# Two attention blocks on one core: scores of a fourth tile ahead of the first values, another pace, a smaller mask, another loop order

## The chip, the core and the metric

The kernel runs on one core of one Trainium2 chip. PE multiplies matrices; VectorE, ScalarE and GpSimd work on vectors; SP issues the DMAs. The metric is the device time in microseconds, the median of several runs. The kernel before takes 1738.6 us (three runs, 1738.31 to 1740.38).

## The reference

Two blocks of attention, each with its own input x (2048 rows of 640) and weights, in float32, 32 heads of 20. Their outputs are put side by side.

```python
# block A: each row attends to 8 rows: itself and those 2, 4, ... 14 before it
idx = pos[:, None] - off[None, :]                 # off = 0, 2, ..., 14
logits = jnp.einsum("bhsd,bhswd->bhsw", q, kg) * scale
logits = jnp.where(mask, logits, -1e9)            # rows before the first are masked
o = jnp.einsum("bhsw,bhswd->bhsd", softmax(logits), vg);  outA = o @ wo
# block B: full attention
p = softmax(jnp.einsum("bhqd,bhkd->bhqk", q, k) * scale)
o = jnp.einsum("bhqk,bhkd->bhqd", p, v);  outB = o @ wo
```

## The kernel before

Every instruction goes through one helper (line 71) that keeps program order, so each engine runs its own instructions in the order in which the program emits them, and all rows of the profile have line 71.

**Stages.** First come block A's projections to q and k (to about 144 us), then block B's (to 281 us, 40 groups of 15 matmuls, lines 590 to 637), then the value projections of both blocks (lines 956 to 998, to about 457 us), during which the first maxima of block B are taken; then the loop over block B (lines 1114 to 1137, 488 steps), a tail of 24 steps, and the last outputs.

**Block A** (lines 329 to 430) has no matmuls in its attention: GpSimd does it. The 2048 rows are 16 tiles of 128. A tile has eight *units*: four of scores (`a_scores`: multiply by q, then add up by halves) and four of values (`a_values`). `UNITS` is the list of (tile, c) in order; c under 4 is a score unit. With `R_AHEAD` = 3 the scores of three tiles come before the first values. Between a tile's scores and values stands its softmax (`a_softmax`), a generator that is moved on by one step per unit (line 417); its maximum and reciprocal run on VectorE, its exponential on ScalarE. Each unit's rows are loaded two units ahead through SP into one of four `akv` buffers (`a_fetch`). Line 412 holds the generator in two cases: while one of the next three units needs value rows that aren't computed yet (`v_rows`), and at a tile's first value unit while two finished tiles wait (`done_a`). Finished tiles are taken from that list in `begin` (line 1033) alone, from step 11 of the loop on.

How much of block A's work is emitted when is set by a running estimate of GpSimd's time, `gp.us`, in which an operation costs 0.2 us and about 2 ns for each column. In the projection of block B, `a_pace` (line 494) is called after each group with `A_SLOW * QK_US * groups` (0.91 x 3.42 us a group), in the value stage with the stage's own estimate (2.2 or 2.72 us a tick), and the loop (line 1037) goes on by 2.36 us a step.

**Row maxima of block B** go through `max_rows` (line 642): VectorE reduces and turns them, GpSimd splits them into two parts (`mtr`), SP stores and loads them.

**The loop over block B** follows a string, `ORDER`. PSUM has eight banks of 512 columns. A token's letter says what is computed and its digits which banks are used. S: two halves of scores, whose exponentials ScalarE takes out of two banks. M: two products for row maxima, reduced by VectorE in one instruction over two adjoining banks (1024 columns). N: the same, reduced in two instructions of 512. Y: one half of scores and one product for maxima. V: one step of the weighted sum of values, every second time with a bank for it. H: a fifth of an output half tile of block A. j: one of five turns of a finished tile of block A on VectorE. A matmul into a bank waits until the instruction that last read that bank has ended.

Of the kernel before, what the change touches and what calls it, by code (L numbers as in the profile page):

```python
# [75 lines left out]
def attention_pair(ctx, tc, xa, wqk_a, wv_a, wo_a, xb, wqk_b, wv_b, wo_b, oa, ob):  # L76
    nc = tc.nc
    PS = bass.MemoryType.PSUM
    const = ctx.enter_context(tc.tile_pool(name="const", bufs=1))
# [937 lines left out]
    def begin(i):  # L1017
# [34 lines left out]
        "S20VY72M3S05Y61V7Y02S35N64VY03N21H65Y74H65S03H65Y72H65Y01H65Y43N72V0S13N46Y75VS41S72N36V0Y13M4S76VS71M2S46V0"
        "Y71S25M3VY71H62Y35H62Y01Y74H62Y35H62Y01H62M3Y75V0S16Y72N34VS15N76S23N40V1Y27S65N43VM6Y05S42V1Y04S73N26VN07S25"
        "H43Y61H43Y02H43Y57H43S06M1H43Y75V0Y16S24N35VY71S62M3Y50V1Y76M3S25VY07H65Y42H65Y70Y13H65Y42H65Y70H65N41V2Y03S74"
        "M5VjM0S73Y46V5jS70jM1S36VY70S14M2V6jS75jM0Y23VY75S04M1S36N75V0S14M2Y76VY15S74M2S60N15V7S64M2Y01VY64S05M2S17N64"
        "V0S15Y23M6VY15M3S27S06N15V2Y70M3S16VY70Y16S53S42N70V1M5S73Y04VM5S72Y34V0Y17S26N54VY71S62Y35Y40Y17V6M2S05Y74VM2"
        "S01H45Y76H45Y03Y21H45Y67H45Y03H45M1Y76V0S53Y74Y12VM3S72Y56V1S07M3Y26VY07M3S25Y61V0S72M3Y56VY71S25M3Y60V7S15M3"
        "Y62VY01M3S56Y27V0Y16M3S52VY71M5S24H03H03Y71H03Y24Y56H03Y71H03S24M5V7Y03S21N65VY06S14M2Y57V6S01jM2Y45VY70M2S14"
        "S56Y70jV1jM2S45Y06VM2S74Y56V0jY71M2jS46VY71M4S63S20N17V6Y52S13Y04VM1S73Y45V0Y17S62N35VY71S64M2S50N17V6Y52M3S01"
        "VY70S15S24N36N07V1S26Y53Y04VM2S75Y46V0Y71S23N65VY74M1S36S50N47V3Y26M4S01VY07M1S64S35N70V6S14M2Y75VY04Y73H21Y65"  # L1060
        "H21S04H21Y37H21Y06H21M4S73N60V2S17M4S36VM0Y73S45V6Y70S12M3VY70S15Y42N36V7S05M1Y34VY06S51M2Y47V0Y16S52M3VY71H26"
        "N35S04H26Y71H26Y03H26Y54H26M0S73V5Y46S70M1VY74S06M1Y35V4Y07M1S63VY07M5S31Y24V7S03jM5Y12VY03M5S41S27Y03jV4jM5"
        "S12Y37VM5S02Y17V3jY04M5jS72VY70S14M5S23N07V1S26Y05M3VS72M5S04Y31V7Y06Y52Y14VN06S53M1S47Y05V6Y43M1S70VY75M3S02"
        "S16N57V0Y14M2S56VY71M4S63S02Y17V6M4S70Y32VM4S70Y12V3Y47M5S02VY70S14M5S23N07V1Y26S05N43VS07Y62H54N31H54S02H54"
        "Y37H54Y60H54M1S73V0S46M1S75VM3S72Y16V5Y07M3S62VY07S61M3Y25V7Y60M3S12VY06M1S53Y47V6Y50S13N24VS70Y15H23N46H23S75"
        "H23Y40H23Y17H23M5Y04V7Y31M5S02VY04M1S35S67N40V3Y21M5S47VY04M1S75Y63V0jS74jM1S56jVjM3S75Y21V6jY70M3S51VY70M1S35"
        "S46N07V3Y24M0S56VY72M4S60S31N27V6Y05M2S41VY70M4S13S26Y07V1M4S72Y36VM4S07Y62V3Y04S75Y21VM0S74Y56V2Y73M0S46VY73"
        "S45Y06N12Y73V4S05Y61N72VS03M5S71Y42V0Y73M5S12VY71M3H25S60H25Y17H25N63S40H25Y17H25S64N03V1Y02M5S73VY07S24M5Y31"
        "V7Y02S64Y53VM0S26Y34V5Y70M1S64VY07S63M1Y45V7Y60M1S34VY06M3S52Y17V6Y05S42N31VM3S70H52Y16H52Y73Y40H52Y16H52Y73"
        "H52M0S46V7Y52S34M0VY62S35S04N17V6jM2S51Y70VjM2S14Y05V7jY61S23M4VjY06M1S35S47jY60V3M1S45Y07VM1S46Y75V0Y14M2S56V"  # L1070
        "Y71S64M2S50N17V6Y52M3S01VY70M1S53S46N07V5Y41M2S06VY70Y61M2S45Y07V6Y51M2S04VY70Y15S42M6Y03S15V4M6S02Y31VS07M5"
        "Y13V2Y04M5S71VY70M3S15Y62V0Y17M3S56VY71M5S24H30H30Y71H30N24S56H30Y71H30S25N64V7Y60M2S14VY06S15M2S47V6Y01S52M3V"
        "M0S75Y43V2Y01M6S35VY01S35Y74Y62V1M3S02Y57VN06S24H73H73M0S25H73Y46H73H73M0S25N46V7S03M1Y45VS06M3S21Y75V0Y62M3"
        "S15VY71S62M3V5jY70S61M3VY07S62S13M4jV0jM6S25jY14jVM6S53Y21V4Y03M6S52VY05M2S71S64N50V7Y61S25M3VY06M1S53S74N60V5"
        "Y71S62M3VY07M1S63S45N70V6Y14S73N52VY70M4S31S26N70V3S24Y51M6VY04M1S57S63Y04V5Y67M1S43VY07S64M1S35V7Y60S41M2VN06"
        "S54H32H32M0S75H32Y46H32H32M0S75Y64V3Y70M1S45VM6S04Y51V2Y03Y74S56VM0S73Y45V6Y70M1S53VY70S54M1H36H36Y70H36Y45Y21"
        "H36Y70H36M4Y21V7S06M2Y45VY06S14M2Y57V0Y16M2S45VY71M4Y63S02V1Y07M4S62VY07M2S64Y51V7Y06M2S45VY06M4S13Y27V6S01jM4"
        "Y32VY70S15M3S26Y70jV1jM3S25Y06VS72jM3jM5S01S72Y34V0Y17M5S42VY71S43M5S20N17V4Y35M1S06VY07M5S31S42N70V3Y41M5S72V"
        "Y70M1S46S35N07V4Y36M1S05VY07M5S31S42N70V3S41M5Y72VS04M5S71N23V0S74M5Y12VY73S41Y56N02V7S61M3Y05VS61M3Y02S57V6M3"
        "S01Y52VM3S70H12H12Y56H12Y07Y34H12Y56H12S07M3V5Y62S01Y43VY07S61M2V4Y05S76M2VY70S15M2Y64V0Y71M2S56VY71M5S42Y30V1"  # L1080
        "Y74S25N63VY07M5S42H31H31Y07H31Y24Y56H31Y07H31M4Y26V0S71M2Y45VY71M2S46S50V7Y61M2S45VjM0S64Y32V5jY06S71N42VY07M3"
        "S61S25jY70V6jM3S21Y05VY74M2jS15V0Y74S16M2VS71M4S63Y20V7S61M4Y03VM1S64Y50Y37S62Y14N05V3S42M6Y01VY24M6S05Y13V2"
        "Y04M6S15VY01M3S57Y62V0S17M3Y56VY71S25M3Y60V7Y15M3S62VY06M1S53S74N60V5Y71S62M3VY07M1S63S45N70V6S14M2Y75VY04Y73"
        "H21Y65H21S04H21Y37H21Y06H21M4S73V0Y12S74M5VS71M2S46Y50V7Y41M2S06VY51S04M2V6Y75S01M2VY70M4S31Y26V0Y73M4S12VY71"
        "M2S64H50H50Y17H50Y64Y32H50Y17H50M3Y62V1S07M5Y43VY07M5S42Y31V0Y72M5S43VjS74jM1S35Y06V7jY14M2S65VY04S16M2V5jY74"
        "S01M2VY07jS61M2S45Y70V6M2S41Y05VY74M2S15V0Y74S16M2VY71S64M2S50Y71V6Y52S43N01VY70Y52S43M0S76Y25V4Y37S01M5VY73"
        "S02M5V1Y73S04M5VY07M2S46S51N70V4Y35M6S21VY05M1S37S64N50V3Y27M5S41VY70M1S46Y35V0Y74S16M2VS71Y64H52N03H52S74H52"
        "Y60H52Y71H52M3S06N17V5S04M2Y61VS07M2S46N15V0S74Y32Y16VM4S73Y62V1Y07M4S32VY07S63M4Y21V7Y06M4S32VY06M2S14H57H57"
        "Y60H57Y41Y23H57Y60H57M1Y43V6S70M4Y12VY70S15M3Y26V7Y05M3S21VY02M5S14S73Y20jV1jY74M5S03VjY72S04M5V3jY72M0jS65V"
        "Y72S64M0S53N27V6Y05S41N23VY70N15Y42S36V7S01S34M5VM0S23Y65V4S70M1Y35VS07M1S36Y54V0Y71M2S46VY71S45M2S60N17V4Y35"  # L1090
        "S62M0VY73M5S20S14N37V2Y01M5S34VY70M3S15S26N07V1M3Y02S56VY07M3H56S21H56Y70H56Y24Y31H56H56N70S42Y31V5Y40S67M1V"
# [114 lines left out]
```

## Time and profile before

| | |
|---|---|
| median of three runs | 1738.6 us (1738.31 to 1740.38) |
| profiled execution, from first to last instruction | 1736.3 us |
| PE busy | 1724.5 us (99%) |
| VectorE busy | 1348.7 us (78%) |
| ScalarE busy | 1338.9 us (77%) |
| GpSimd busy | 1266.2 us (73%) |
| granted TensorE clock, mean | 0.999 of full speed |
| mean DMA rate | 143 GB/s |

The page gives no other time of the profiled execution than its span. In the profile DVE is VectorE, ACT is ScalarE, POOL is GpSimd, PEld is PE's loading of weights. Matmuls are pipelined and their ends are modelled, so a busy PE isn't PE at its peak; what PE waits for is seen best at its weight loads. A group's busy time leaves out overlaps between its instructions, its mean does not.

### The profile page before, as it was taken

The page shows a single profiled execution, that of the slowest core. Times are in us where ns is not written, and L with a number is a line of the kernel's source. Part 1 is how long each engine was busy: PE and PEld are TensorE (multiplying, and loading weights), DVE is VectorE, ACT ScalarE, POOL GpSimd, SP SyncE. Part 2 cuts the span into 40 slices and gives each one's busy share as a digit, 9 for nine tenths or more (in the row PEclk, how much of TensorE's full clock was granted, in tenths as well). Part 3 has the DMA queues.
Part 4 walks back from the last instruction along what each step waited for, and adds up shares of the span by engine and source line. Part 5 has one row for each costly group of instructions (what it writes and reads, how often), then busy time and mean ns, then how long its engine had stood idle before and what let it go on. Part 6 is the DMA issues. An engine that isn't in the chain of part 4 may idle for free.

```text
span 1736.3 us, 34687 instructions
## 1 busy us (share of the span) xinstructions
PE 1724.5 (99%) x12711; PEld 1006.0 (58%) x12711; DVE 1348.7 (78%) x1825; ACT 1338.9 (77%) x2658; POOL 1266.2 (73%) x1122
## 2 busy tenths in 40 slices
...
GB/s 227 119 139 239 304 261 273 259 204 187 199 151 125 96 161 153 93 136 158 135 95 173 126 119 127 170 135 88 158 143 106 147 95 61 46 36 53 33 76 113
DMA packets 194436, 248.29 MB, mean 143 GB/s; under 512 B 89309, under 2 KB 114397, under 8 KB 193273
## 3 DMA queue, kind: packets, MB, share of 16 engines
...
## 4 chain that ended last, share of the span: by engine, by line
PE 90%; POOL 4%; DVE 2%; ACT 1%; DMA 1%; issue 1%; SPq 0%; POOLq 0%; ACTq 0%; DVEq 0%
PE ps_st L71 90%; POOL akv L71 2%; DVE mx L71 1%; ACT e L71 1%; POOL xn L71 1%; DMA stg<-wv_b 0%; SPq L71 0%; POOL ww L71 0%; POOL xl L71 0%; POOL ao L71 0%; ACT more L71 0%; DMA vb_d<-ve 0%; POOL al L71 0%; DMA s_d<-sm 0%; DMA rb<-s_d 0%
## 5 line engine op out<-in xcount | busy, mean ns | idle before, releaser
L71 DVE TENSOR_REDUCE mx<-ps_st 128x1 f32<-128x512 f32 (+1 forms) x1504 | 1227.6, 875 | 57.3 <-PE ps_st L71 47.8
L71 ACT ACTIVATE e<-ps_st 128x512 f32<-128x512 f32 x2048 | 1066.7, 627 | 30.7 <-PE ps_st L71 16.8
L71 PE MATMUL ps_st<-bk,bq 60*128 60x512 f32 x2048 | 553.4, 436 | 1.0 <-ACT ve L71 0.5
L71 PE MATMUL ps_st<-bq,bk 62*128 62x512 f32 x2048 | 548.7, 433 | 5.6 <-ACT ve L71 3.0
L71 PE MATMUL ps_st<-e,vb 128*32 128x512 f32 x4096 | 543.0, 604 | 0.4
L71 PEld LDWEIGHTS ps_st<-bq,bk 62*128 62x128 f32 x2048 | 274.8, 184 | 403.3 <-ACT e L71 246.5
L71 POOL TENSOR_TENSOR braw<-braw,more 128x512 f32<-128x512 f32 x224 | 288.2, 1287 | 85.5 <-ACT more L71 85.1
L71 PEld LDWEIGHTS ps_st<-bk,bq 60*128 60x128 f32 x2048 | 257.1, 184 | 108.7 <-DVE mx L71 61.2
L71 POOL TENSOR_TENSOR akv<-akv,aq 128x1280 f32<-128x1280 f32 x64 | 188.9, 2951 | 166.4 <-DVE w L71 166.3
L71 POOL TENSOR_TENSOR akv<-akv 128x640 f32<-128x640 f32 (+3 forms) x304 | 282.2, 928 | 14.4
L71 ACT COPY ro<-ps_st 128x320 f32<-128x320 f32 (+2 forms) x172 | 73.7, 463 | 171.1 <-PE ps_st L71 122.7
L71 PE MATMUL ps_st<-ww,xn 64*128 64x320 f32 (+1 forms) x1776 | 187.1, 309 | 0.0
L71 PEld LDWEIGHTS ps_st<-ww,xn 64*128 64x128 f32 (+1 forms) x1776 | 175.7, 186 | 14.6 <-ACT e L71 8.3
L71 PEld LDWEIGHTS ps_st<-e,vb 128*32 128x32 f32 x4096 | 82.1, 108 | 149.0 <-issue 75.4
L71 POOL TENSOR_TENSOR akv<-akv,al 128x1280 f32<-128x1280 f32 x64 | 151.6, 2368 | 0.2
L71 ACT COPY more<-ps_st 128x512 f32<-128x512 f32 x224 | 136.3, 609 | 3.5 <-PE ps_st L71 1.5
L71 PE MATMUL ps_st<-xn,w 128*128 128x512 f32 x480 | 115.8, 390 | 0.0
L71 PEld LDWEIGHTS ps_st<-xn,w 128*128 128x128 f32 x480 | 90.1, 188 | 19.3
L71 ACT CAST pr<-ps_st 128x512 fp32r<-128x512 f32 x40 | 23.5, 587 | 98.8 <-PE ps_st L71 96.0
L71 PE MATMUL ps_st<-ww,aot 64*128 64x320 f32 x960 | 99.7, 308 | 0.0
L71 DVE TENSOR_TENSOR pr<-ps_st,pr 128x512 fp32r<-128x512 f32 x40 | 27.6, 691 | 86.7 <-ACT pr L71 86.7
L71 PEld LDWEIGHTS ps_st<-ww,aot 64*128 64x128 f32 x960 | 90.3, 186 | 5.8 <-POOL ao L71 0.6
...
## 6 DMA issues: line engine op xcount, KB each, us to landing
akv<-ka_d SPq DMA_DIRECT2D x128, 320.0 KB
akv<-va_d SPq DMA_DIRECT2D x128, 320.0 KB
...
rb<-s_d SPq DMA_DIRECT2D x128, 64.0 KB
```

The costliest lines, as they stand in the source:

```text
L71: return self.tc.keep_in_program_order(op(*a, **k))
```

## The change

The list `UNITS` has the scores of four tiles (16 units) before the first values; from tile 2's values on it is as before. For that the buffer `al` of scores has four copies in place of three, and the mask is kept once for all heads and broadcast in the addition. While the unit's index is under `EARLY` = 16, each softmax takes two steps per unit. `A_SLOW` is 0.78. The string `ORDER` is another one with as many steps (V 488), S-halves (1952) and maxima products (1840); H stands at the same steps, j mostly one step earlier. S goes from 625 to 634 tokens, M from 440 to 349, N from 129 to 229, Y from 702 to 684.

```diff
@@ -50,7 +50,7 @@
 AHEAD = 2.4
 QK_US = 3.42
 V_US = 2.72
-A_SLOW = 0.91
+A_SLOW = 0.78
 A_FROM = 1
 
 
@@ -310,10 +310,10 @@
         pe.transpose(warm[:, :128], ident, ident)
     give(warm)
 
-    mask = const.tile([128, WIN, H], F32, name="mask")
+    mask = const.tile([128, WIN], F32, name="mask")
     gp.memset(mask, 0.0)
     gp.affine_select(out=mask, in_=mask, compare_op=ALU.is_ge, fill=NEG, base=-PAD,
-                     pattern=[[1, WIN], [0, H]], channel_multiplier=1)
+                     pattern=[[1, WIN]], channel_multiplier=1)
     ones = [sb.tile([128, 16 * VC + 11], F32, tag=tag, bufs=3 if tag == "raw" else 2, name="ve")
             for tag in ("raw", "rb", "raw", "rb")]
     for t in ones:
@@ -326,7 +326,10 @@
 
 
 
-    UNITS = [(t, c) for k in range(NT + R_AHEAD) for t, cs in ((k - R_AHEAD, range(4, WIN)), (k, range(4))) if 0 <= t < NT for c in cs]
+    EARLY = 4 * R_AHEAD + 4
+    UNITS = [(t, c) for t in range(R_AHEAD + 1) for c in range(4)] + [
+        (t, c) for k in range(R_AHEAD, NT + R_AHEAD) for t, cs in ((k - R_AHEAD, range(4, WIN)), (k, range(4)))
+        if R_AHEAD < t < NT or cs[0] for c in cs]
     v_rows = [0]
     a_kv, a_t = {}, {}
 
@@ -351,7 +354,7 @@
 
     def a_scores(t, c, kv):
         if c == 0:
-            a_t[t][1] = sb.tile([128, WIN, H], F32, tag="al", bufs=R_AHEAD, name="al")
+            a_t[t][1] = sb.tile([128, WIN, H], F32, tag="al", bufs=R_AHEAD + 1, name="al")
         q, L, _ = a_t[t]
         pool(kv, kv, q.unsqueeze(1).to_broadcast([128, 2, D]), ALU.mult)
         yield
@@ -364,7 +367,7 @@
 
         _, L, _ = a_t[t]
         if t % (NT // 2) == 0:
-            pool(L, L, mask, ALU.add)
+            pool(L, L, mask.unsqueeze(2).to_broadcast([128, WIN, H]), ALU.add)
         yield
         yield
         m = sb.tile([128, 4, H], F32, tag="am", bufs=2, name="am")
@@ -415,7 +418,8 @@
             for d in done_a:
                 d[0] -= 1
             for g in soft.values():
-                next(g, None)
+                for _ in range(2 if n < EARLY else 1):
+                    next(g, None)
             if c == 4:
                 run_jobs(soft_jobs, 1)
                 for _ in soft.pop(t):
@@ -1044,66 +1048,67 @@
 
 
     ORDER = (
-        "Y07S61M2Y45V0Y71S26M3Y05V7Y06M3S52Y71V0Y26M3S75VY71M5S24S03N17V2Y06S15Y34VM0S74Y56V3Y70S21N46VY70M4S12S63N07V1"
-        "Y26M4S03VY07M2S64S51N70V6Y52S73N41VY70S52M3Y16V7Y05S42Y31VM4S06Y12V3jY07M4S26VjY70M1S64S53V0M6S14Y25VjM6S13M4"
-        "S20V1jY27S63jM4VY07M2S64S51N70V6Y52M3S71VY70M1S53S46Y07V5jM1S74Y63VjM1S07M3S65S02jY71jV6jM3S50Y12VM3Y70S52V1"
...
-        "S31N70V2S36M4Y71VY03M4Y76S12V0Y71M4S32VY71M2Y64S05Y17V6Y05M2S41VY70Y15S42Y36S07N15V4M1S36Y50VM1S73Y06")
+        "S51N24N73Y60V5Y17Y64Y02S53V1Y03M6S45Y21V0Y43M5S27VY31S24M6S05N31V2S04Y76Y35VM0S46Y57V3Y14N20S67VY42M6S15S03N42"
+        "V1Y06M4S73VY07M2S64S51N07V6S45M2Y10VY75M3S12Y06V7Y52S14Y03VjM5S32Y41V0jY56N37S21VY25S61M3S07V2jM5S13Y04VM6S13"
+        "M4jS20V1Y27S63M4VjY20M3S65S17N20V6Y13M4S27VY30M1S76S54Y30jV7jY12M5S40VY23Y41S75jS60M2Y41V7M5S32Y01jVM4Y26S31j"
...
+        "S72M5Y40V1Y32M5S70Y34VS23M6N51S04V2S36Y07M4VS31M6Y03S25N41S67V0M3S26Y15VM3S71Y06")
```

## Rows read from the trace of the kernel before

**Rows 1.** Windows view: busy us of each engine in stretches, then granted clock, DMA share, GB/s

```profile
core 0: us, PE busy (x) PEld busy (x) DVE busy (x) ACT busy (x) POOL busy (x), PEclk, DMA share, GB/s
...
470.00:1600.00 1130.00, 1127.94 (x8412) 510.60 (x8408) 1100.99 (x1543) 1098.26 (x2202) 995.84 (x879) 1.00 0.42 120
...
240.00:303.00 63.00, 63.00 (x354) 55.33 (x354) 21.55 (x29) 22.66 (x38) 3.81 (x8) 1.00 0.84 272
...
400.00:450.00 50.00, 46.56 (x541) 42.72 (x538) 38.82 (x38) 10.89 (x25) 48.51 (x35) 1.00 0.68 207
```

**Rows 2.** Waits view, 470 to 1600 us: total us, times, longest us

```profile
DVE mx L71 <- PE ps_st L71: 18.5, 66, 1.0
...
ACT e L71 <- PE ps_st L71: 16.5, 48, 0.9
...
PEld ps_st L71 <- ACT e L71: 314.2, 506, 0.9
...
PEld ps_st L71 <- DVE mx L71: 170.3, 346, 0.9
```

**Rows 3.** Timeline, GpSimd, 235 to 302 us: start, us, instructions, [idle before <- releaser]

```profile
235.78 2.96 POOL L71 TENSOR_TENSOR akv<-akv,aq 128x1280 f32<-128x1280 f32 x1
...
238.82 3.47 POOL L71 TENSOR_TENSOR akv<-akv 128x640 f32<-128x640 f32 x4
...
242.37 0.32 POOL L71 TENSOR_TENSOR al<-akv 128x64 f32<-128x64 f32 x1
...
301.69 4.76 POOL L71 TENSOR_TENSOR xn<-stg,xn 128x1024 fp32r<-128x1024 f32 x2 [58.88 <-ACT xn L71]
```

**Rows 4.** Timeline, GpSimd: first instruction on tile 2's values

```profile
486.68 2.37 POOL L71 TENSOR_TENSOR akv<-akv,al 128x1280 f32<-128x1280 f32 x1
```

**Rows 5.** Timelines of VectorE, GpSimd, SP and ScalarE, 431 to 449 us

```profile
431.48 0.21 DVE L71 STREAM_TRANSPOSE mtr<-mx 128x32 f32<-128x32 f32 x1
...
437.55 2.95 POOL L71 TENSOR_TENSOR akv<-akv,aq 128x1280 f32<-128x1280 f32 x1
...
440.44 0.21 POOL L71 CAST mtr<-mtr 128x32 fp32r<-128x32 f32 x1
...
444.47 1.79 SPq L71 DMA_DIRECT2D vb_d<-ve  x4
...
447.65 0.43 ACT L71 COPY ve<-ps_st 128x320 f32<-128x320 f32 x1 [7.43 <-DMA vb_d<-ve]
```

**Rows 6.** Waits view of SP and PE, 400 to 460 us

```profile
SPq L71 <- POOL mtr L71: 7.4, 1, 7.4
...
PE ps_st L71 <- ACT ve L71: 3.4, 2, 3.0
```

**Rows 7.** Timelines of SP, ScalarE, VectorE and PE, 284 to 301 us

```profile
284.91 5.21 SPq L71 DMA_DIRECT2D stg<-xa  x3
...
294.48 1.05 ACT L71 CAST xn<-stg 128x1024 fp32r<-128x1024 f32 x1 [4.06 <-DMA stg<-xa]
...
298.00 0.69 DVE L71 TENSOR_TENSOR xl<-stg,xl 128x512 fp32r<-128x512 f32 x1
...
298.69 2.38 PE L71 MATMUL ps_st<-ww,xn 64*128 64x320 f32 x24
```

**Rows 8.** Timeline, VectorE: a softmax maximum, and pairs of reductions in a run

```profile
229.00 0.63 DVE L71 TENSOR_REDUCE am<-al 128x32 f32<-128x256 f32 x1 [3.76 <-POOL al L71]
...
412.56 2.36 DVE L71 TENSOR_REDUCE mx<-ps_st 128x2 f32<-128x1024 f32 x2 [0.31 <-PE ps_st L71]
...
1016.76 1.82 DVE L71 TENSOR_REDUCE mx<-ps_st 128x2 f32<-128x1024 f32 x2 [0.17 <-PE ps_st L71]
```

**Rows 9.** Groups by form, whole run: busy us, mean ns of one, idle before

```profile
L71 DVE TENSOR_REDUCE mx<-ps_st 128x2 f32<-128x1024 f32 x544 | 657.0, 1216 | 31.5 <-PE ps_st L71 29.8
...
L71 DVE TENSOR_REDUCE mx<-ps_st 128x1 f32<-128x512 f32 x960 | 619.8, 681 | 25.8 <-PE ps_st L71 18.0
...
L71 POOL TENSOR_TENSOR al<-al,am 128x256 f32<-128x256 f32 x32 | 23.6, 739 | 0.0
...
L71 POOL TENSOR_TENSOR al<-al,mask 128x256 f32<-128x256 f32 x2 | 1.5, 733 | 0.2
```

More of the change, by code (lines that the diff above doesn't have):

```diff
@@ L1052, in attention_pair @@
[L1052 to L1091, printed above, removed]
@@ new lines, in attention_pair @@
+        "V1Y06M4S73VY07M2S64S51N07V6S45M2Y10VY75M3S12Y06V7Y52S14Y03VjM5S32Y41V0jY56N37S21VY25S61M3S07V2jM5S13Y04VM6S13"
+        "M4jS20V1Y27S63M4VjY20M3S65S17N20V6Y13M4S27VY30M1S76S54Y30jV7jY12M5S40VY23Y41S75jS60M2Y41V7M5S32Y01jVM4Y26S31j"
+        "V0Y27M3S56VY17S62M4S30Y17jV6jM3Y25S70VM1S43Y70V5jY42S36M0VjS72M3S16Y50V7jN14Y32S60VY15S34H06N27H06S51H06Y32H06"
+        "Y57H06N14S23V7Y60N51S42VY46N53S02V7Y61M4S02VN06S31H25Y47H25Y03H25Y61H25Y70M3H25Y61V0Y57S64M2VY16M4S72Y03V1Y72"
+        "N64S05VY70N36S52Y41V7S50M2Y64VY10N23H56Y74H56S10H56Y27H56Y31H56Y04N27V3S16N50Y24VY17S56Y20V3Y45M6S01VS20N54S17"
@@ new lines, in attention_pair @@
+        "V3Y65Y02Y14VY57H62N10S43H62Y75H62Y41H62Y03H62M4Y71V0S67M2Y45VY71Y64S32N50V7S41Y36N52VY01N64S53V7Y10N62S53VN50"
+        "S16H43Y27H43Y15H43Y60H43Y71H43N56S20V7Y42N31S65VY20M5S43Y71V2Y03S46N57VN30S14H65Y72H65Y31H65N04H65H65M2S71V0j"
+        "Y45N67S12VjM4jS36Y12V7S36M4S01VY23M5S40jV1jS72M3Y56VY07M4S32S61N07V3S24M5Y10VY27M4S60S13N27V6S10M4Y32VY71S03M4"
+        "S26N71V0Y53S42M6VY54M2S16S07N54V1Y60M2S57VY65Y47S13S20N65V4S13N76Y52VY01N36S57V2Y45M0S37VY35Y64Y10S27Y35V6M0"
+        "S24Y57VM2S01H45Y67H45N03S12H45Y76H45Y01H45M2Y76V0S54M1S73VM5S47Y12V3Y46N75S02VY10S74M5Y32V1Y07M4S36VY20M6S35"
@@ new lines, in attention_pair @@
+        "Y41V2Y03N67S54VY03M4S61Y72V0Y16M3S57VY51N26S74H30H30N15S72H30Y46H30Y71H30N25S46V7Y24S31M5VjY04S21M5Y37V0Y21M4"
+        "S63VY76M2S14S50jY67jV1M3S25Y70VjS56M3Y27V0Y61M3S52VY17S62jM4Y03Y71V6S45N20S73VM4S27Y10V3Y65N74S20VY72M5S40S31"
+        "N72V4Y05M6S31VY30Y12S67Y45N30V1S26N57S43VY50S24M6V3Y10N52S67VY40M6S53S12N40V5Y71M3S26VY27M0S63S45N27V6S01M3Y25"
+        "VY07Y34H21Y65H21S07H21Y64H21Y03H21M4S76N03V2S15N47S06VM4Y13S70V6Y21M4S73VY72S01Y43N65V7S10M2Y64VY05S62N13Y47V0"
+        "S12M5Y34VY71H62N35S04H62Y17H62Y30H62Y45H62N13S70V4Y65N12S37VY03M6S15Y42V0Y31S76M4VY12M6S43Y50jV2Y17S36M4VY31"
@@ new lines, in attention_pair @@
+        "S76jM4S20Y13jV7M5S24Y03VS41jM5Y20V3Y41M6S52VY40M1S56S37N40jV5S61M2Y74VS17Y30M5S42V1Y30N74S56VY53M6Y24S01Y53V2"
+        "Y67M0S45VY76M4S32N10S67V3Y24M5S17VS10Y42Y36Y57Y12V0Y73N65S24VY17S26N34V5Y70N23S16VY04M6S15S23N40V1S25M6Y43VS02"
+        "Y76H54N13H54S06H54Y21H54Y73H54N10S26V7S43N52S10VM5S12Y43V0Y75S61N23VY42M5S71Y30V2Y41S57N63VY45S67M0Y32V4Y75N61"
+        "S03VS50Y76H32N14H32S56H32Y17H32Y04H32M6Y51V4Y30M5S72VY10M2S76S54N10V7Y26S31M4VY60M1jS43Y75V0S41jM2S67jjVM4S23"
+        "Y61jV7Y45M2S01VY64M0S37S25N46V3Y72M0S54VY27M4S61S30N27V6Y13M4S20VY73S12M4S60Y73V1S65Y24N03VS46N57Y02V3S15N47"
@@ new lines, in attention_pair @@
+        "S60VM1S75Y64V0Y31S72N54VY31S72M5Y40Y31V7S26M4Y03VS62M0S45Y73V6N40Y12S35VM0S47H52Y63H52N41S07H52Y63H52Y40H52S71"
+        "N63V4Y07M5S23VY71S32M5Y04V7Y13S26Y05VM2S16Y45V0Y72S13N65VY21M3S76Y05V2Y71S63N40VY61M4S37Y20V6Y37S45M1VM3S70H52"
+        "Y61H52N74S30H52Y16H52Y73H52N40S16V7Y32S45M0VY62S54S10N73jV6M4S27Y13jVM4S70Y32jV1Y47N56S02VY04S32M6Y15S04jV3jM1"
+        "S76Y50VM6S24Y15V0Y24Y73Y61VY72M3S61S50N27V6Y51M3S02VY50M1S73Y46Y05V7Y21M3S06VY02Y16M4Y37S02V1Y36M4S02VS03M6Y25"
+        "Y04Y31S67V2Y05S43N61VS54M6Y30V2Y41N56S73VY01M3S57Y26V0Y71M4S32VN61S27Y45H30H30Y62Y17H30Y45H30Y26H30Y74Y15V2Y67"
@@ new lines, in attention_pair @@
+        "S03M4VS01M6Y43S25V0S76Y14N23VY45N67S12V3Y54S60M1VY47S60S25N13V4S01M6Y32VY50Y61H73H73Y24N05H73S16H73N42H73S10"
+        "N56V7Y43N12S05VS04N61S53Y72V0Y14M5S32VjY17S43N26V5Y17S02M3VY06S71M3S52jjV0jM6S14Y35VM1S67Y43jV5Y02M6S13VY04M1"
+        "S75S63N40V7Y51S62M3VY60M1S57S43N06V5Y21S70M3VY67M0S25S43N67V2Y50S16M3VY15M6S02N43S15V0Y21S76M4VY13Y60S24S75N13"
+        "V6Y14N70S32VY41S35S27N60V4S63N15Y20VN16S57H32H32N40S15H32Y67H32H32M0S45Y67V3Y14N50S27VY64S21N57V0Y43Y25S16VM3"
+        "S25Y71V6Y24N03S51VY07M1S45H36H36Y07H36Y54Y21H36Y70H36M4Y21V7S06M2Y54VY10S56M2Y47V1Y65S20N43VY67M4Y20S31V6S72M3"
@@ new lines, in attention_pair @@
+        "Y51VY70S32M4Y61V7Y02M3S56VY21M5S04Y37V1jY40S65M2VY40M6S53S12jY40jV5M6S31Y02VN73S64S25jM6S01Y34jV2M6S50Y14VY07"
+        "M5S42S13N07V4Y56M1S03VY50M6S32S41N05V3Y24M6S01VY54M1S06S37N45V0Y16M3S27VY52M6S14N30S52V1S76M4Y23VM6S05N42S13V0"
+        "S71M5Y43VY71S64Y52N30V7S46M1Y35VS60M3Y12S57V6M3S01Y25VN40S37H12H12N56S34H12Y07H12Y53H12S46N07V5S13N24S70VY21"
+        "S67M3V0Y52S16N43VY45S12M6Y30V4Y21M6S53VY15M2S07Y64V1Y70N23S56VY07M5S24H31H31Y70H31Y42Y56H31Y07H31M4Y26V0S37M1"
+        "Y45VY76N31S42S05V7jM3S62Y01VM4S23Y61jV0Y27N43S51VY72M4S61S30Y72jjV6M3S51Y20VY57M3jS12V0Y56S17M3VS51M6S34Y20V5"
@@ new lines, in attention_pair @@
+        "N63S17Y40VM2S14N07S51S62Y43N50V1S32M6Y54VY32S50M6Y14V3Y20M6S51VY02M4S17Y63V0S17M4Y26VY71S32M4Y06V7Y12M3S50VY25"
+        "M0S64S73N25V6Y10S74M2VY15S40M2S76N15V4S30N72Y16VS73N50H21Y64H21S73H21Y65H21Y07N34H21S65V0Y23M6S41VS23M4Y16S70"
+        "V2Y35N14S76VY37N01S65V4Y03Y27Y65VY01M2S75Y64V0Y17N35S26VY17M2S64H50H50Y17H50Y64Y32H50Y17H50M3Y62V1S50M6Y43VY20"
+        "M5S47Y31V2Y74N60S35VjS74M5S13Y02V7jY56jN41S32VY36N50S42V1Y67M4S32VY07M2S64S51Y07jjV6M3S25Y17VM3S25Y10V7Y26M4"
+        "S31VY32Y10S45N67S32V1Y56S04N73VY52N04S61S53Y72Y60V1Y32S45N07VS04M2Y56V7Y10S23M4VY10M2S47S65N01V4Y23M6S05VY01M2"
```

35 lines of the change are left out of this document (19 added, 16 removed).

## The prediction

> **What bounds the kernel now.** I read the page's busy shares first, then the stages by windows, then who waits for whom. PE looks full on the page from end to end, but PE's ends are modelled; the stages tell more. From 470 to 1600 us, the loop over block B, VectorE and ScalarE are both busy over 97% (1100.99 and 1098.26 of 1130 us), GpSimd 88% [rows 1]. There PE's weight loads stand still for 314.2 us on ScalarE's exponentials and for 170.3 us on VectorE's maxima: PE waits for a PSUM bank to come free. The two evicting engines themselves starve little: VectorE 18.5 us, ScalarE 16.5 us [rows 2]. So the loop's time is the eviction work of two engines with equal load, and an order can win back at most those waits. Before 300 us PE is full in every window (63.00 of 63 us, 240 to 303) and GpSimd nearly empty (3.81 us); at 400 to 450 us PE loses 3.4 us, and GpSimd is full (48.51 of 50) [rows 1].
>
> **The change part by part.**
>
> *Four more score units in block A's front.* The list of units is a list of (tile, c). Before, the first value unit stands at index 12, and the look-ahead of three holds the generator at index 10 until value rows exist; after, these are 16 and 14. So four units go into the gap of GpSimd, which ends its tenth unit at 242.7 us and stands idle for 58.88 us [rows 3]. A unit is 2.96 + 3.47 + 0.32 us and its gaps, some 6.9 us [rows 3]: 4 x 6.9 = 27.6 us fit in. GpSimd isn't on the path there, so this gains nothing by itself; what counts is where the lead is spent. Only tile 3's scores and tile 0's values change places: from tile 2's values on the list is the same. And tile 2's values are held by another gate: two finished tiles may wait, and the first is taken away only at step 11 of the loop. In the trace those values begin at 486.68 us, right behind work queued by then [rows 4]. So the lead ends in that gate, and the loop gets block A's work at the steps it had. The order string bears that out: each of its 160 output tokens H stands at the same step as before.
>
> What is left of the lead is at the seam. The turned maxima of a row block are ready on VectorE at 431.7 us, but GpSimd splits them only at 440.44, behind three value units' work and the first multiply of tile 4 (437.55, 2.95 us). SP stands 7.4 us before that store, the value rows' stores behind it issue at 444.47, the copy into their buffer waits 7.43 us, and PE 3.4 us [rows 5, 6]. After, at this point in the program index 28 is due, not 24, which is tile 2's first value unit: held. The multiply of 2.95 us leaves the queue ahead of the split. I take -2.9 us (from -3.4, the whole wait of PE, to 0, if the units fall otherwise).
>
> *The pace 0.78.* 14 units of about 6.5 us in the program's own estimate, with three softmaxes, are some 96 us; at 0.78 x 3.42 = 2.67 us a group from the fifth group on, they last to about group 39 of 40; before, at 3.11 us, ten units ended at group 25. GpSimd then has gaps between units: free. The loads are not so surely free: four units of 2 x 320 KB and a query tile are 2.9 MB, 11 us at the 272 GB/s of 240 to 303 us, and most now fall between 240 and 281. The DMA engines are busy 0.84 of that stretch [rows 1], which leaves 0.16 x 41 = 6.6 us before 281. The next stage has no slack there: its second x block is cast when its load lands (ScalarE waits 4.06 us for it), VectorE ends the split at 298.69, and PE starts on it at 298.69 [rows 7]. By the pace the last of the new loads issue near 270 us, and that x load at 284.91 [rows 7], so I take 0; bounds 0 and +4.4 us (11 us of loads less 6.6 free).
>
> *Two steps of softmax per unit until index 16.* The same instructions, sooner. The maximum on VectorE now follows GpSimd's last add at once, not a unit later: each of three tiles can hold VectorE by up to one unit, 6.9 us, more than the 3.76 us it shows now [rows 8]. Behind it stands the eviction of the projection; PE goes round 8 banks at 3.44 us a group, 27 us, so a wait of 10 us is covered: 0. Without that cover it would be 3 x 6.9 = 21 us, which nothing here makes likely, as VectorE is busy 21.55 of 63 us there [rows 1].
>
> *The mask with one value for all heads.* Two adds on GpSimd of 733 ns; the subtraction of the maximum, which has a broadcast operand of the same kind, takes 739 [rows 9]: 0 (bounds of a few tenths either way, on an engine with idle time).
>
> *The loop's order.* I counted the tokens. Per step it has the same exponentials and the same maxima. But pairs of maxima reduced together (M) go from 440 to 349, pairs reduced apart (N) from 129 to 229, mixed pairs (Y) from 702 to 684: 91 reductions of 1024 fewer, 182 of 512 more. Alone they last 1216 and 681 ns [rows 9], which would be 182 x 0.681 - 91 x 1.216 = +13.3 us. In a run they overlap: two of 1024 are 2.36 us, a 1024 and a 512 are 1.82 (a merged row names its first form alone; the length tells the other) [rows 8], so the next costs 2.36 - 1.22 = 1.14 and 1.82 - 1.22 = 0.60: 109.2 - 103.7 = +5.5 us of VectorE. I take 5.5, since VectorE nearly always has a next one here; ends: 0 (all in its 18.5 us of waits) and 13.3.
>
> The Trainium skill (Perfetto Trace Analysis, Optimizing Scalar/DVE Operations) speaks against this edit: it gives VectorE about 125 ns of fixed cost for each operation on PSUM and advises larger operations where the engine is saturated. By it, as an estimate, 91 more instructions would be +11.4 us; the rows of this trace give 60 ns each, and the trace decides.
>
> Against the 5.5 stands when banks come free. For each use of a bank I counted, in the string, how many evictions stand on the same engine behind the one it must wait for; with none or one, the engine is nearly empty when PE gets its bank. Behind VectorE this falls from 611 uses to 445 (-27%), behind ScalarE it rises from 211 to 257 (+22%). A PE held by VectorE starves ScalarE, and the reverse: I scale 16.5 us by -27% and 18.5 by +22%, -4.5 on ScalarE and +4.1 on VectorE. VectorE's side is then 5.5 + 4.1 = +9.6, ScalarE's -4.5. Both follow one program, and neither leads now; I take the middle, +2.5 us.
>
> **Sum.** Against the profiled span: 1736.3 - 2.9 + 0 + 0 + 0 + 2.5 = 1735.9. The median of the runs, 1738.6, is 2.3 above the span; so 1738.2 us: no change that can be measured (0.2% is 3.5 us, about what this kernel's runs can tell apart).
>
> **The rivals.**
> 1. *Finer releases pay: faster.* Each pair reduced apart frees its first bank 1.216 - 0.681 = 0.535 us sooner; 91 times, 48.7 us. If a quarter ends up in PE's path, -12 + 5.5 - 2.9 = -9.4: 1729.2 us. For it: PE's 170.3 us behind VectorE [rows 2]. Against: only 35 us of starving are there to win.
> 2. *VectorE becomes the bound: slower.* It decides from the point where VectorE's starving falls under half of ScalarE's: then its whole side counts, +9.6 - 2.9 = +6.7: 1745.3 us; with the reductions at their lone durations, 1753. For it: 1100.99 against 1098.26 us busy, no reserve [rows 1]. Against: VectorE still starves 66 times [rows 2].
> 3. *The x load of the next stage lands late: slower.* +4.4 + 2.5 - 2.9: 1742.6 us. For it: no slack [rows 7]; against: the new loads should be issued 15 us before.
> 4. *The split of the maxima stays where it was.* Then the seam's 2.9 us stay and the order decides: 1741.1; it is inside the forecast's own range.
>
> **How the numbers follow.** The forecast gets 0.40, with its own range 1734 to 1742; rival 1 0.30, rival 2 0.22, rival 3 0.08. Faster by over 0.2% (under 1735.1): rival 1 and 0.05 of the forecast, 0.35. Slower (over 1742.1): rival 2, most of rival 3 and 0.02 of the forecast, 0.28. Within: 0.37. The range goes to the centres of rivals 1 and 2 and a little past them: 1728 to 1747.
>
> **What would show it.** Right: GpSimd's gap of 58.88 us shrinks by some 27; tile 2's values still begin near 480 to 487 us, with GpSimd idle shortly before; the split of maxima stands near 437 us and PE's wait on the copy falls under 1 us; from 470 to 1600 VectorE's busy time rises by some 5 us, and PE waits less for VectorE and more for ScalarE. Wrong: block A's output tiles come earlier in the loop; PE stands still at 298 us; VectorE's busy time rises by 11 us or more; or the loop is shorter by more than 5 us, which would mean that PE's bank waits, not the eviction work, set it.

## The result and the profile after

The changed kernel takes 1741.6 us (median of 21 runs, 1740.38 to 1742.31) against 1739.17 us for the kernel before in the same runs (21, 1738.2 to 1740.38): a ratio of 1.0013, interval 1.0007 to 1.0019. That is +2.4 us: less than the 0.2% that I had set as the limit, but on the slow side by a margin that these runs resolve. I had put the forecast 0.4 us below the kernel before. The profiled executions, one of each kernel, have spans of 1736.3 and 1739.6 us, 3.3 us apart.

I cut both traces at the same events: the first product for block B's maxima, the first value projection of the last part ahead of the loop (there begins what I call the seam), the loop's first value product, the last turn of maxima on VectorE, and the last copy. The first maxima product comes right behind PE's first matmuls on the second x block, at 298.69 us before; below I call that point the start of the value stage.

| stretch | before | after | difference | forecast |
|---|---|---|---|---|
| start to first maxima product (x load) | 301.20 | 308.06 | +6.86 | 0 (0 to +4.4) |
| value stage, to the seam | 138.63 | 138.51 | -0.12 | 0 |
| seam, to the loop's first value product | 18.64 | 13.34 | -5.30 | -2.9 (-3.4 to 0) |
| loop, to the last turn | 1162.68 | 1164.50 | +1.82 | +2.5 |
| tail | 111.68 | 111.65 | -0.03 | 0 |
| sum | | | +3.23 | -0.4 |

The windows view after, beside [rows 1]: the loop and the seam look as forecast, and the new row, 303 to 308 us, is where the time went.

```profile
core 0: us, PE busy (x) PEld busy (x) DVE busy (x) ACT busy (x) POOL busy (x), PEclk, DMA share, GB/s
240.00:303.00 63.00, 58.69 (x300) 51.12 (x299) 23.25 (x28) 19.37 (x32) 34.95 (x37) 0.99 0.93 300
303.00:308.00 5.00, 4.25 (x29) 4.12 (x31) 0.79 (x2) 3.66 (x7) 1.18 (x1) 0.50 0.99 366
400.00:450.00 50.00, 50.00 (x609) 47.04 (x607) 43.19 (x40) 10.45 (x24) 39.58 (x36) 1.00 0.49 149
470.00:1600.00 1130.00, 1128.34 (x8398) 505.22 (x8395) 1104.67 (x1631) 1097.72 (x2199) 990.01 (x871) 1.00 0.43 120
```

From 240 to 303 us PE, full before, is busy 58.69 of 63 us, and the DMA share is up from 0.84 to 0.93. From 400 to 450 us the lost 3.4 us are back. From 470 to 1600 us VectorE has 3.7 us more, but such a window cuts the two loops at different places. Over the whole loop, before and after, between the events of the table:

```profile
458.47:1621.15 1162.68, 1159.18 (x8621) 522.60 (x8621) 1132.58 (x1588) 1129.99 (x2264) 1009.27 (x890) 1.00 0.42 119
459.91:1624.41 1164.50, 1161.93 (x8619) 518.77 (x8621) 1138.07 (x1676) 1131.21 (x2264) 1001.32 (x880) 1.00 0.43 118
```

VectorE is busy 5.5 us more, ScalarE 1.2 us more.

Timelines after at the start of the value stage (SP, ScalarE, VectorE, PE, GpSimd), beside [rows 7] and the last row of [rows 3]:

```profile
290.77 3.28 SPq L71 DMA_DIRECT2D stg<-xa  x3
299.60 1.04 ACT L71 CAST xn<-stg 128x1024 fp32r<-128x1024 f32 x1 [9.24 <-DMA stg<-xa]
303.27 1.61 ACT L71 COPY ro<-ps_st 128x320 f32<-128x320 f32 x4 [0.82 <-DMA va_d<-ro]
303.11 0.69 DVE L71 TENSOR_TENSOR xl<-stg,xl 128x512 fp32r<-128x512 f32 x1
303.75 3.98 PE L71 MATMUL ps_st<-ww,xn 64*128 64x320 f32 x24 [5.05 <-ACT ro L71]
306.82 2.39 POOL L71 TENSOR_TENSOR xn<-stg,xn 128x1024 fp32r<-128x1024 f32 x1 [29.75 <-ACT xn L71]
```

The chain reads from the top. The x block that SP issued at 284.91 before is issued at 290.77; ScalarE, an in-order engine, stands 9.24 us for it (4.06 before) with four copies of the projection behind the casts; PE needs the banks that these copies free, and stands still for 5.05 us. The 24 matmuls behind the wait then take 3.98 us in place of 2.38, at a granted clock of 0.50 from 303 to 308 us: the 1.2 GHz level, after PE had stood still. 5.05 + 1.60 is 6.65 of the 6.86 us. GpSimd's gap has shrunk from 58.88 to 29.75 us, as forecast.

SP's loads of block A's keys after, 235 to 290 us; before, there is none in this stretch:

```profile
238.43 1.29 SPq L71 DMA_DIRECT2D akv<-ka_d  x2
...
249.63 1.37 SPq L71 DMA_DIRECT2D akv<-ka_d  x2
...
256.15 1.26 SPq L71 DMA_DIRECT2D akv<-ka_d  x2
...
266.42 1.03 SPq L71 DMA_DIRECT2D akv<-ka_d  x2
...
275.77 1.32 SPq L71 DMA_DIRECT2D akv<-ka_d  x2
```

Five pairs, each a 128 x 1280 tile of 655 KB. Four of them are more than the kernel before loads ahead of the x block, one only comes later. And the DMA share in slices of 10 us, first before, then after:

```profile
250.00:260.00 10.00, 10.00 (x45) 8.22 (x44) 2.84 (x4) 2.39 (x4) 0.00 (x0) 1.00 0.85 306
260.00:270.00 10.00, 10.00 (x46) 8.28 (x45) 4.00 (x6) 3.37 (x6) 0.00 (x0) 1.00 0.74 235
270.00:280.00 10.00, 10.00 (x45) 8.21 (x44) 2.75 (x4) 3.42 (x5) 0.00 (x0) 1.00 0.94 291
...
250.00:260.00 10.00, 10.00 (x46) 8.21 (x45) 3.10 (x5) 2.39 (x4) 9.29 (x12) 1.00 1.02 388
260.00:270.00 10.00, 10.00 (x46) 8.29 (x45) 6.40 (x7) 3.58 (x6) 9.53 (x10) 1.00 0.89 307
270.00:280.00 10.00, 10.00 (x45) 8.18 (x44) 2.82 (x4) 3.48 (x5) 6.67 (x9) 1.00 1.00 293
```

Before, the shares are 0.85, 0.74 and 0.94: the transfers had room in two of the slices. After, they are 1.02, 0.89 and 1.00, with little room left.

The seam, first PE before, then after GpSimd, PE and twice GpSimd, beside [rows 4 to 6]:

```profile
449.77 3.41 PE L71 MATMUL ps_st<-ww,xn 128*128 128x320 f32 x12
...
440.61 0.21 POOL L71 CAST mtr<-mtr 128x32 fp32r<-128x32 f32 x1
452.68 2.03 PE L71 MATMUL ps_st<-ww,xn 128*128 128x320 f32 x12
466.33 0.72 POOL L71 CAST ww<-stg 128x640 fp32r<-128x640 f32 x1 [25.18 <-PE ps_st L71]
482.21 2.37 POOL L71 TENSOR_TENSOR akv<-akv,al 128x1280 f32<-128x1280 f32 x1
```

The split of the maxima stands at 440.61, where it stood before, but the value stage now runs 6.7 us later and the turn on VectorE with it (438.26), so it lags the turn by 2.4 us, not 9. PE's wait of 3.4 us is gone, and with it a stretch of slow matmuls: before, the 12 behind that wait took 3.41 us (granted clock 0.53 from 449.8 to 453.2 us); now such a group takes 2.03. Tile 2's values begin at 482.21 with GpSimd idle for 25.18 us up to 466.33, so block A's lead ends in the gate that I had named.

Waits in the loop after, 470 to 1600 us (total us, times, longest), beside [rows 2]:

```profile
PEld ps_st L71 <- ACT e L71: 308.3, 581, 0.9
PEld ps_st L71 <- DVE mx L71: 166.1, 265, 0.9
ACT e L71 <- PE ps_st L71: 16.6, 55, 0.7
DVE mx L71 <- PE ps_st L71: 14.4, 51, 0.7
```

VectorE starves 4.1 us less than before, ScalarE as much as before. Over the whole loop VectorE's 5.5 us of added work come out of 3.7 us of its idle time and 1.8 us of a longer loop.

### The profile page after: what moved, and what is told of

The parts are those of the page before. It is cut to its first block, busy times and chain, and to the rows that moved or that the text cites. A ratio compares the mean times of both kernels' runs of the same rounds, so it can differ in the third digit from the quotient of the medians.

```text
span 1739.6 us, 34834 instructions
## 1 busy us (share of the span) xinstructions
PE 1726.5 (99%) x12711; PEld 1001.3 (58%) x12711; DVE 1361.5 (78%) x1916; ACT 1340.2 (77%) x2658; POOL 1268.0 (73%) x1122
## 4 chain that ended last, share of the span: by engine, by line
PE 89%; POOL 4%; DMA 3%; ACT 2%; issue 1%; DVE 1%; SPq 0%; POOLq 0%; ACTq 0%; DVEq 0%
PE ps_st L71 89%; POOL akv L71 2%; ACT e L71 1%; DMA stg<-wv_a 1%; POOL braw L71 1%; DMA bq<-qb_d 1%; POOL ww L71 1%; DMA va_d<-ro 0%; ACT more L71 0%; DVE mx L71 0%; DMA akv<-ka_d 0%; SPq L71 0%; DMA stg<-xa 0%; POOL ao L71 0%; DMA akv<-va_d 0%
## 5 line engine op out<-in xcount | busy, mean ns | idle before, releaser
L71 PE MATMUL ps_st<-bq,bk 62*128 62x512 f32 x2048 | 559.1, 435 | 1.3 <-ACT more L71 0.4
L71 PE MATMUL ps_st<-bk,bq 60*128 60x512 f32 x2048 | 545.0, 434 | 0.7 <-ACT e L71 0.4
L71 PE MATMUL ps_st<-wc,xn 128*128 128x512 f32 (+1 forms) x432 | 90.5, 355 | 0.4 <-ACT xn L71 0.4
```

Of the source, the lines that this page charges most:

```text
L71: return self.tc.keep_in_program_order(op(*a, **k))
```

## The experiments

All ratios are to the kernel before on the same chip (medians 1739.13, 1739.23 and 1739.47 us in the three sets of runs), with their intervals.

**The front without the order, and the order without the front.** The changed kernel with the old string, and the kernel before with the new one:

```diff
     ORDER = (
-        "S51N24N73Y60V5Y17Y64Y02S53V1Y03M6S45Y21V0Y43M5S27VY31S24M6S05N31V2S04Y76Y35VM0S46Y57V3Y14N20S67VY42M6S15S03N42"
...
+        "Y07S61M2Y45V0Y71S26M3Y05V7Y06M3S52Y71V0Y26M3S75VY71M5S24S03N17V2Y06S15Y34VM0S74Y56V3Y70S21N46VY70M4S12S63N07V1"
...
```

> The changed kernel with the old loop order: block A's front alone. Theory T (three terms, read from the two traces): the first row-tiled value matmul starts 5.1 us late because its x block lands late and the first 4 us behind the wait run at a granted clock of 0.50, together +6.8 us; the seam before the loop gives 5.4 us back; the loop adds +1.8 us. Front alone: +6.8 - 5.4 = +1.4 us against the kernel before. Rival R1 (the order is the whole change): 0 us. Rival R2 (the front is the whole change): +2.4 us or more.

Measured: 1741.15 us, 1.0013 [1.0003, 1.0022], +2.0 us. PE waits 4.9 us at the start of the value stage and the seam is 13.17 us long: both large terms belong to the front alone.

> The kernel before with the new loop order alone. Theory T: the loop's term alone, +1.8 us, with VectorE busier by some 6 us in the loop and no wait of PE at 298 us. R1 (the order is the whole change): +2.4 us. R2 (the front is the whole change): 0 us.

Measured: 1743.61 us, 1.0027 [1.0016, 1.0038], +4.5 us: a miss. In the profiled execution the loop is 2.5 us longer, which is the term that I had forecast, and the seam 1.8 us longer (20.44). The two parts don't add: 2.0 + 4.5 is 6.5, and together they cost 2.4.

**Two units fewer ahead of the value rows.** The generator is held at its 12th unit instead of its 14th, with the new order and with the old:

```diff
-            while any(u[1] >= 4 and v_rows[0] <= u[0] for u in UNITS[n:n + 3]) or c == 4 and len(done_a) > 1:
+            while any(u[1] >= 4 and v_rows[0] <= u[0] for u in UNITS[n:n + 5]) or c == 4 and len(done_a) > 1:
```

> The changed kernel, but block A is held two units sooner in the projection stage (after 12 units, with loads up to unit 13), so that 1.3 MB less is loaded there. Theory T (the DMA engines were full, so the x block came late): the last loads of block A are issue near 260 us, x lands some 3 to 5 us sooner, PE's wait at 298 us falls from 5.1 to 0 to 2 us: -4 to -6.8 us against the changed kernel if the seam keeps its gain. Rival S (the seam won only because the value stage began later): what is won at 298 us is lost at 445, about 0 us in all.

Measured: 1736.09 us, 0.9984 [0.9975, 0.9992]: 3.0 us under the kernel before and, by the two ratios, some 5 us under the changed one; with the next run it is the fastest of all. Its loads of keys in 235 to 290 us, its x load, ScalarE's cast and PE's start:

```profile
238.38 1.30 SPq L71 DMA_DIRECT2D akv<-ka_d  x2
...
249.65 1.06 SPq L71 DMA_DIRECT2D akv<-ka_d  x2
...
256.06 1.27 SPq L71 DMA_DIRECT2D akv<-ka_d  x2
...
284.65 4.54 SPq L71 DMA_DIRECT2D stg<-xa  x3
294.22 1.05 ACT L71 CAST xn<-stg 128x1024 fp32r<-128x1024 f32 x1 [3.91 <-DMA stg<-xa]
298.87 2.46 PE L71 MATMUL ps_st<-ww,xn 64*128 64x320 f32 x24 [0.22 <-ACT ro L71]
```

Three pairs of loads, none issued after 257 us, and the x load is on time: PE waits 0.22 us and keeps its clock. At the seam of the same kernel, GpSimd's split and PE's wait on the copy:

```profile
438.51 0.21 POOL L71 CAST mtr<-mtr 128x32 fp32r<-128x32 f32 x1
...
PE ps_st L71 <- ACT ve L71: 0.4, 1, 0.4
```

The value stage starts on time here and the seam is still only 14.13 us long, with PE waiting 0.4 us. So the seam's gain doesn't come from the late value stage: twelve units of lead are enough for it.

> The changed kernel with the generator held two units sooner and with the old loop order. Theory T2 (the seam's gain and the order's cost are separate terms): the seam stays short, -4.5 us against the kernel before, and without the new order's +0.5 to +2.5 us the run is 1734 to 1735.5, under the 1736.1 of the run with the new order. Rival (the new order fits the new front and pays there): 1736.5 or more, slower than with the new order.

Measured: 1736.53 us, 0.9983 [0.9973, 0.9992], above the 1734 to 1735.5 that I expected and at the edge of the rival's range. But it is not slower than with the new order, as the rival has it: with this front the new order is worth nothing either way that these runs resolve, as the two ratios agree within their intervals. PE waits 0.55 us at the start of the value stage.

**One unit fewer.**

```diff
-            while any(u[1] >= 4 and v_rows[0] <= u[0] for u in UNITS[n:n + 3]) or c == 4 and len(done_a) > 1:
+            while any(u[1] >= 4 and v_rows[0] <= u[0] for u in UNITS[n:n + 4]) or c == 4 and len(done_a) > 1:
```

> The changed kernel held at 13 units (14 in the change, 12 in the run that beat it). Theory T (the DMA engines' load decides): PE's wait at 298 us lies between the 0.2 us of 12 units and the 5.1 us of 14, some 1.5 to 3 us, and the time between 1736 and 1741.6, about 1738.5. Rival P (a single thing, the last unit's buffer wait or load just ahead of the x load, decides): as with 12 units, under 0.5 us of wait and 1736 us.

Measured: 1739.48 us, 1.0 [0.9991, 1.0009]. Its loads stand where the changed kernel's do, without the last one at 275.77; PE's start:

```profile
301.39 3.13 PE L71 MATMUL ps_st<-ww,xn 64*128 64x320 f32 x23 [2.65 <-ACT ro L71]
```

This makes a row of doses. Ahead of the x block, two, three and four pairs of key loads more than in the kernel before go with 12, 13 and 14 units, and PE waits 0.22, 2.65 and 5.05 us. Two further pairs fit; the third and the fourth cost 2.4 us each, and 2.4 us is what a pair's 655 KB last, as an estimate, at the 272 GB/s of that stretch [rows 1]. The last slice ahead shows it too: from 270 to 280 us the DMA share is 0.91, 0.99 and 1.00 (0.94 before, without a wait).

**The x load first in its queue.** SP issues the x block ahead of the four loads that stand before it:

```diff
                     elif g8 == 6:
+                        xraw = x_raw(1)
                         for _ in range(4):
                             q_loads.pop(0)()
-                        xraw = x_raw(1)
```

> The changed kernel with the x block's load issued ahead of the four query loads that stood 6.9 us on SP's queue. Theory T: x issues at 283 to 285 us and not at 290.8, PE's wait at 298 us vanishes: -6.8 us against the changed kernel (1734.8) if the seam keeps its gain. Rival S (the seam won only because the value stage began later): -6.8 + 5.4 = -1.4 us. Rival Q (bandwidth, not the place in the queue, delays the load): no change at 298 us, and the query loads come late as well, 0 or slower.

Measured: 1741.08 us, 1.0011 [1.0002, 1.002]: my expectation missed. SP, ScalarE and PE in this kernel:

```profile
280.69 7.41 SPq L71 DMA_DIRECT2D stg<-xa  x3
...
297.59 1.05 ACT L71 CAST xn<-stg 128x1024 fp32r<-128x1024 f32 x1 [0.83 <-DMA stg<-xa]
302.12 1.61 ACT L71 COPY ro<-ps_st 128x320 f32<-128x320 f32 x4 [2.96 <-DMA va_d<-ro]
302.59 3.64 PE L71 MATMUL ps_st<-ww,xn 64*128 64x320 f32 x24 [4.38 <-ACT ro L71]
```

Issued 10.1 us sooner, the block is cast 3.3 us sooner (second cast, 300.89 in the changed kernel), with the DMA engines at 0.99 from 281 to 290 us (0.80 in the changed kernel); then the copies behind the casts wait 2.96 us for the stores of the value rows, which come later for it. PE's wait shrinks by 0.67 us. So another place in the queue doesn't help: what stands last is late. That fits a stretch with too many bytes in it, though this run alone doesn't show it.

**The pace and the softmax steps.** The pace of the kernel before, which emits block A's work sooner, a pace that emits it later, and the changed kernel with one softmax step per unit:

```diff
-A_SLOW = 0.78
+A_SLOW = 0.91   # second kernel: 0.70
```

```diff
-    EARLY = 4 * R_AHEAD + 4
+    EARLY = 0
```

> The changed kernel with the old pace 0.91, all else as changed. GpSimd shows no gap at 0.78 from 170 to 277 us, so it can't end sooner. Theory T: the loads are asked for sooner and wait on SP for a free buffer, ahead of the projection's stores; the bytes before 281 us are the same: PE's wait at 298 us stays 3 to 7 us, 1740 to 1744 us. Rival F (the pace put the last loads too late): the wait falls under 2 us, 1736 to 1738.

Measured: 1742.49 us, 1.0018 [1.0009, 1.0026]. The time is in theory T's range, but the mechanism isn't T's: PE doesn't wait at all at the start of the value stage, which was rival F's sign. The loss comes earlier. Waits from 160 to 310 us:

```profile
DVE am L71 <- POOL al L71: 14.1, 3, 8.5
DVE am L71 <- POOL am L71: 11.5, 2, 8.3
PE ps_st L71 <- DVE w L71: 5.9, 2, 3.2
```

VectorE stands up to 8.5 us in softmax steps that wait for GpSimd. Behind them in its queue is the splitting of block B's weights (`w`), and for these PE waits 5.9 us. The cover of 27 us that I counted is one of PSUM banks; it is none where PE waits for weights. The value stage starts 7.85 us later than in the kernel before, and the last pair of loads is issued 25 us ahead of the x block, not 15. As many pairs go ahead of the x block as in the changed kernel, but with more time to land. This run can't tell whether the longer time or the earlier loads spared the x block.

> The changed kernel with a pace of 0.70. By the program's own estimate the 14 units no longer fit into 40 groups; one or two, with their loads, move into the value stage. Theory T: fewer bytes before the x load, so PE's wait at 298 us falls to 0 to 2 us, and the time to 1736 to 1738, as with the hold at 12. Rival L (what comes late weighs more): the loads stand directly ahead of the x load on SP, the wait grows over 5 us.

Measured: 1743.15 us, 1.0022 [1.0013, 1.0031]: missed. SP's one pair of key loads behind the x block, ScalarE and PE:

```profile
296.23 1.26 SPq L71 DMA_DIRECT2D akv<-ka_d  x2
...
303.21 0.63 PE L71 MATMUL ps_st<-ww,xn 64*128 64x320 f32 x1 [2.66 <-ACT ro L71]
304.72 1.21 ACT L71 COPY ro<-ps_st 128x320 f32<-128x320 f32 x3 [1.56 <-DMA va_d<-ro]
305.20 3.56 PE L71 MATMUL ps_st<-ww,xn 64*128 64x320 f32 x23 [1.36 <-ACT ro L71]
```

One pair moves behind the x block (issued at 290.64), so as many go ahead of it as in the kernel held at 13 units, and PE's first wait is as long as there, 2.66 us for 2.65. That is what the doses say. But the moved pair now stands in SP's queue between the stores of the value rows (295.01 and 298.00), ScalarE's copies wait 1.56 us for these stores, and PE another 1.36 us. A third wait of 1.35 us, at 283 us, is for VectorE's split of the x block before. So a load put behind the critical one can hold up the next transfer that an engine waits for.

> The changed kernel with one softmax step per unit throughout, as before the change. Theory T (the loads' bytes decide): VectorE and SP wait some us less on block A's maxima near 200 to 260 us, but PE's wait at 298 us stays 4 to 6 us: -1 to 0 us. Rival D (the double step holds VectorE, and with it the projection's stores on SP, and so the x load): the wait falls under 2 us, -4 us or more.

Measured: 1740.07 us, 1.0004 [0.9996, 1.0013]. PE still waits 4.26 us:

```profile
302.98 3.72 PE L71 MATMUL ps_st<-ww,xn 64*128 64x320 f32 x24 [4.26 <-ACT ro L71]
```

So the two steps per unit are not the cause of the late x block; at most 0.8 of its 5.05 us could be theirs.

**The seam's cause by itself.** The kernel before, with the split of the maxima taken from GpSimd:

```diff
         def parts():
+            if loop[0] is None:
+                act.copy(mt[:, 1], raw)
+                dve.tensor_tensor(mt[:, 2], raw, mt[:, 1].bitcast(F32), ALU.subtract)
+                return
             gp.tensor_copy(mt[:, 1], raw)
```

> The kernel before, but before the loop the turned maxima are split by ScalarE and VectorE, not by GpSimd; block A's front and the order are the old ones. Theory G (the seam's loss hangs on the split standing behind block A's units on GpSimd): the split follows the turn at 431.7 us at once, SP's 7.4 us wait and PE's 3.4 us vanish with the low clock behind them, -4.5 to -5.4 us (1733.8 to 1734.7). Rival L (the loss hangs on the DMA load near 440 us, the stores landing late): PE still waits 2 to 4 us there, 0 to -1 us.

Measured: 1738.27 us, 0.9995 [0.9986, 1.0004]. The seam falls from 18.64 to 13.06 us: its wait and the slow stretch behind it were indeed the price of standing behind block A on GpSimd. But the value stage gets 3.9 us longer. ScalarE's and VectorE's part of the split, and PE's wait:

```profile
434.72 0.22 ACT L71 CAST mtr<-mtr 128x32 fp32r<-128x32 f32 x1 [2.33 <-DVE mtr L71]
434.97 1.19 DVE L71 TENSOR_TENSOR mtr<-mtr 128x32 fp32r<-128x32 f32 x1 [0.28 <-ACT mtr L71]
...
PE ps_st L71 <- DVE mx L71: 2.3, 4, 0.6
```

Three times in this stage VectorE now waits for ScalarE's copy and does a subtraction, with its reductions queued behind, and PE waits 2.3 us in all for the banks that these reductions read (its weight loads 4.7 us).

**Maxima reduced apart, by themselves.** The kernel before with 91 of its 440 joint pairs reduced one by one on the same banks, spread evenly, and with all 440 (the start of the second kernel's string is shown):

```diff
     ORDER = (
-        "Y07S61M2Y45V0Y71S26M3Y05V7Y06M3S52...
+        "Y07S61N23Y45V0Y71S26N34Y05V7Y06N34S52...
```

> The kernel before with 91 of its 440 pairs M, evenly spread, reduced apart (N on the same two banks), nothing else moved. Theory V (VectorE has no reserve): +5.5 us. Theory H (half, the two engines sharing it): +2.7 us. Rival Z (freeing the first bank sooner pays for the extra instructions): 0 or faster.

Measured: 1741.02 us, 1.0011 [1.0001, 1.002], +1.8 us, the loop +2.2, nearest to theory H.

> The kernel before with all 440 pairs M reduced apart. 440 x 0.06 = 26 us more of VectorE. Theory V: +26 us or a little less. Theory H: +13 us. Rival Z: under +5 us.

Measured: 1748.98 us, 1.0056 [1.0042, 1.007], +9.8 us, the loop +9.0, between rival Z and theory H. The windows view over the whole loop, beside the one above:

```profile
461.04:1632.71 1171.67, 1167.62 (x8620) 519.09 (x8621) 1151.22 (x2025) 1134.21 (x2264) 1008.83 (x888) 1.00 0.42 118
```

VectorE is busy 18.6 us more than before, 42 ns for each further reduction where I had taken 60 from pairs in a run, and about half of it, 20 ns each, comes out in the loop's length. Finer releases don't pay: both kernels are slower.

## Why the prediction was wrong

**The x load, the step that failed.** I had bounded it by "0 and +4.4 us (11 us of loads less 6.6 free)" and took 0, because "the last of the new loads issue near 270 us". It was the other end: a wait of 5.05 us. The working of that bound was sound, as the doses show (two pairs fit, each one beyond costs its own 2.4 us); the reason to leave it wasn't. The last load issues at 275.77, 15 us ahead of the x block, but between 270 and 280 us the DMA engines had been at 0.94 before the change, so a load "before 281" was not a free one. Rival 3, which I gave 0.08, is what happened (in the 0.28 for slower I counted half of it, not most). That its 1742.6 us stands 1.0 from the 1741.6 measured is in part luck, with two errors of opposite sign in it: the wait's price left out the slow stretch behind it (1.6 us), and the seam's gain was too small. It is luck too that the forecast was off by so little: against the x load's +6.86 us stood a seam 2.4 us better than forecast and an order 0.7 us cheaper.

**The pace.** "GpSimd then has gaps between units: free" was wrong: GpSimd is busy 9.29 and 9.53 of 10 us from 250 to 270 and works up to 277 us. I had stretched the units over the groups by the program's own estimate and not asked whether GpSimd keeps up.

**The seam.** Right in sign and cause, too small: -5.30 for -2.9. The wait of 3.4 us went whole, and the slow matmuls behind it gave another 1.4, which [rows 6] doesn't show: a wait of PE had a second price behind it, at both places of this change. I also misread what stood ahead of the split: between the turn and it came one value unit (431.92 to 437.60) and the multiply, not three units. The split itself did not move to 437 us as I said it would; the value stage moved. That the gain is real without this is shown by the kernel held at 12 units. There the split is only 1.9 us sooner, and so are the value rows' stores (442.52, not 444.47); the copy that waits for them starts 2.1 us behind their issue (444.66), not 3.2 (447.65). Together that is the 3.0 us by which PE's wait falls. Before, a pair of block A's loads stands in SP's queue between the split and those stores (442.78), there none does; that this makes the landing slower is argued, not tried.

**The loop.** +1.82 for +2.5, VectorE's time +5.5 as forecast, PE's waits on VectorE down 4.2 as the count of banks had it, but its waits on ScalarE not up. One trace is no scale for 2 us: over four profiles with the old string (the kernel before, the front alone, 12 units with the old order, the split moved to VectorE) the loop takes 1162.7 to 1164.8 us, mean 1163.9; over eight with the new one 1163.9 to 1165.5, mean 1164.8. The order's cost in the loop is then about 1 us; the two kernels with more pairs reduced apart, too, are only 1.0 and 7.8 us over that mean. (The stretch up to the first maxima product spreads likewise, 301.0 to 302.7 us over five profiles with the old front; the 308.06 after is far outside.) The new order adds 1.8 us to the seam of the old front: PE's wait there is 4.0 us in place of 3.4, and the low clock lasts longer (granted 0.60 from 453 to 456 us, 0.93 before). The new front has no such wait, and the order adds nothing to its seam. Why the wait itself grows by 0.6 stays open; the kernel with all pairs split, whose first steps change too, has a wait of 4.3 and a seam of 20.55 us. By the Trainium skill (Perfetto Trace Analysis, Optimizing Scalar/DVE Operations), with its 125 ns for each operation, 440 more would be 55 us, as an estimate; the measured 18.6 us of VectorE and 9.8 us of the kernel decide. Its advice to prefer larger operations agrees in sign.

**Softmax steps and mask.** Nothing, as forecast, at pace 0.78 (one step per unit is 1.5 us faster, with intervals that overlap). The mask's add takes 615 ns in place of 733 [rows 9].
